# Block-recurrent attention and feed-forward: token weights of the reading through DRAM in 5 transfers instead of 16 moves

## The chip, the cores and the metric

One Trainium2 chip; the program runs on one core. The metric is device time in microseconds of one execution, here the median over runs. The core has TensorE (PE; its weight loads, PEld, overlap its matmuls), VectorE (DVE), ScalarE (ACT), GpSimd (POOL) and SyncE (SP). SyncE computes nothing here: it issues DMAs, one after another, and an issue that has to wait holds up all that come after it. SBUF is the on-chip memory of 128 rows (partitions), PSUM holds what TensorE writes (eight banks), DRAM is outside.

## The reference

Two parts, the first giving the input of the second. B, H, S, Ns, D are 8, 8, 512, 32, 64; the feed-forward has d_model 512 and d_ff 2048. All is float32; the two weights come as float64.

```python
def _attn_ref(x, state):
    scale = 1.0 / np.sqrt(D)
    scores = scale * np.matmul(x, state.transpose(0, 1, 3, 2))
    a = softmax(scores)                        # over the 32 states
    xread = np.matmul(a, state)                # (B, H, S, D)
    scores2 = scale * np.matmul(state, x.transpose(0, 1, 3, 2))
    a2 = softmax(scores2)                      # over the 512 tokens
    sread = np.matmul(a2, x)                   # (B, H, Ns, D)
    return np.concatenate([xread, sread], axis=2)

def _moe_ref(x, w_in, w_out):                  # x: (B * 544, 512)
    h = x @ w_in
    sp = np.maximum(h, 0.0) + np.log1p(np.exp(-np.abs(h)))
    g = h * erf(sp)
    return g @ w_out
```

(The softmax is written out in the reference, with the row maximum taken off and 1e-9 added to the sum.) The second softmax, a2, gives each token a weight for each state; `sread` is the *reading* of this document: for each head, 32 weighted sums over 512 tokens.

## The kernel before

The work is cut by batch and by half of d_ff. In the first half of the run (units A, one per batch, then SA for the rows of `sread`) the first 1024 columns of d_ff are done, in the second half (units B and SB) the other 1024; B adds to what A stored. Batch 0 goes by a path of its own at the front, with small pieces that start as soon as data is there. The products of a unit are cut into quarters and done with seven products instead of eight (a Strassen scheme, in B with a second level), which is why there are so many sums on VectorE: `hidden` (L623) makes the unit's first products, `second` (L675) and `inner` (L734) the second ones, softplus and erf are on ScalarE, the sums are in `sums_a`, `sums_y`, `inner_sums` and `mixed`.

The attention's `xread` is never formed: its weights `a` stay as the unit's right factor (`y`), and `mixed` (L575) multiplies the states with w_in instead. The reading is formed, as states' rows for SA and SB.

The attention of batches 1 to 7 is written in `attention(b)`. All of its work is on tiles inside `at`, with heads paired (h = 2i + e):

- Loads `xq` (two DMAs per head) bring x so that 32 x 32 block transposes on VectorE (`tx`) give it with the channel on the rows. `s` (L493) forms the scores of all heads in two PSUM banks, row = 32 i + state, column = token; ScalarE copies them to `sc` (`c0`, `c1`).
- First softmax: block transposes `tu`, maximum `mx`, `sb`, exp `ex`, sum `sm`, `iz`, `nm`, and transposes back, `ta`, into `y`.
- Second softmax: maximum `my` and `ms`, exp `ey` with its sum, into `both[:, 2 + e]`; `iy` takes the sums' inverse. Then `ty0` and `ty1` transpose the weights block by block into `both[:, 0:2]`: after it a row is 32 i + (token mod 32), and the columns are (e, c, m, n): half, group c of 128 tokens, m (which 32 of them) and state n.
- The product needs a token on each of 128 rows. So the blocks have to move between rows: the block at rows 32 i, columns m goes to rows 32 m, columns i, of `a2T`. Sixteen DMAs from SBUF to SBUF do it, `z00` to `z33` (L534), 32 rows x 8 runs of 32 floats each, 32 KB.
- `x0` to `x7` (L298) load x itself for the product, one DMA per head, into `x_n` (row = token in the group, columns = group, head, channel).
- `read(b)`: `rd` (L467) multiplies, 32 states x 64 channels per matmul, over the four groups of tokens; `rn0`, `rn1` (L475) scale by the sums' inverse; `rt` transposes, `rc` copies into `sT`.

Batch 0 (`attention0`) fills `a2T` from PSUM with the copies `tw0c` and `tw1c`.

`sums_y` also puts `y` and its sums in DRAM for the second half (`kept_y`, L551, 512 KB, and `kept_sy`, L553). The weights' columns are loaded as float64 and put together from their words in `piece` (`i0` to `i7`, `o0` to `o7`), the later ones in between the A units.

The order of everything is written out: `ORDER` is a list of some 2,400 step names. Each step emits its instructions when its name comes up, and each engine runs its own instructions in that order, SyncE's DMA issues too. Names: `a3z12` is step z12 of batch 3's attention, `A2p10` a second product of unit A2, `rd3` the reading of batch 3, `~7*11` eleven small matmuls into bank 7 that compute nothing and keep TensorE busy.

Of the kernel before, what the change touches and what calls it, by code (L numbers as in the profile page):

```python
# [8 lines left out]
F32 = mybir.dt.float32  # L9
# [8 lines left out]
warm lx0 lst0 lx2 lx1 lx3 i0l0 lst8 lst5 lst3 lst7 lst4 lst1 ~7*11 x0 lst2 s0 lst6 x0c i1l1 x2 s0c  # L18
i1l0 i0l1 x1 i2l0 i2l1 x3 x1c i3l1 x2c i3l0 q0 x3c q01c q1 i0a0 q00c big0 tm0 i0a1 i0v0 q10c q11c
i0v1 ~7*1 tm1 max0 u0 i0v2 max1 o0l0 n00 u1 less0 less1 exp0 big1 exp1 sum0 sum1 i1a0 inv0 inv1  # L20
norm0 i1a1 big i1v0 ~4*16 ta0 n00c0 norm1 i0+a0 i1v1 ta0c ~7*1 ta1 i0+a1 n00c1 ta1c i1v2 wt1 i0+v0
wt0 ~6*6 n02 i0+v1 n02c0 i2a1 i0+v2 n02c1 o0l1 ~7*5 n01 i2a0 h0 o1l1 n01c1 u1c o1l0 n01c0 a1xq0
i2v0 h1 i2v1 a1xq1 h0s i3a0 i2v2 h2 h0c i3v0 h1c o2l1 i3a1 u0c o2l0 n10 a1xq2 h3 n10c1 h1s i3v1
n10c0 h2c o0a0 h4 i3v2 h2s wz h3c o3l1 wn0 n12 o3l0 o0a1 h5 wn1 a1xq3 n12c1 h3s o0v0 a1xq5 n12c0
y01 tw1 o0v1 a1xq4 tw0 h0e a1xq7 y02 h6 o0v2 tw1c a1xq6 tw0c h0g o1a0 rd0 a1tx0 o1a1 o10 rn0 a1x5
o1v0 h2e a1x3 o1v1 a1x4 i4l1 rt0 o2a1 o00 o1v2 o2a0 o20 h2g o2v0 h4s o22 o2v1 h4c o3a1 o2v2 h7
o3a0 a1tx1 h5s o3v0 o02 h6s y04 rc0 h5c a1tx2 yl0 h7s o3v1 o12 a1tx3 h4e o3v2 a1s h4g a1c1 a2xq7
a1c0 a1tu1 h7c i4l0 o04 a1tu0 h6c a1x0 i5l0 h6e a1mx1 i5l1 a1mx0 A1m0 a2xq4 a1sb1 o24 a2xq5 a1sb0
a1ex1 a1my1 a1ex0 a2xq0 a1sm1 A1m01 o14 a1x2 a1sm0 A1m00 a2xq1 a1iz h6g i4a0 a1x6 A1m1 a2xq2 i4a1
a1nm0 o06 a1my0 a2xq3 A1m10 a1ta0 A1m11 a2xq6 a1ms a1nm1 a1ey1 A1f01 y11 a1ey0 A1M1 o26 a1ta1  # L30
A1f0c o0c A1M2 i5a1 A1f05 y12 A1M3 A1f06 a1ty0 y13 A1f02 A1f0u2 a1ty1 A1f07 A1M4 A1f0c11 a1z23
i4v0 a1z02 A1f11 A1f0u3 a1z03 y14 i4v1 a1z11 A1f04 a1z22 a1z01 o30 A1f0c22 A1f0s11 a1z20 i4v2
a1z13 A1f0c21 A1f1c A1f03 A1f0s22 i4k a2tx3 a1z12 A1f0s12 A1f16 a1x1 A1f0c12 A1f12 a1x7 A1f1u2
a1iy T1 a1z33 A1f0s21 A1f17 a1z10 A1f1c11 a1z21 a2tx0 A1f15 a1z32 A1f1u3 a2tx1 a1z31 A1f1s11 A1f14
A1f1c22 a1z00 i5a0 a1z30 y03 A1f13 a2tx2 yk0 A1f1c21 i5v0 yl1 o32 A1f1s22 i6l0 A1f1c12 A1f1s12
i5v1 rd1 T2 A1e0 rn10 a2x0 rn11 i5v2 rt1 i6l1 rc1 a2x7 a2s A1g0 A1f1s21 o34 a3xq0 a2c1 a2c0 a3xq2
a2tu0 o36 a3xq4 a2tu1 A1e1 a2mx0 i7l1 A2m0 a2mx1 a3xq7 a2sb0 o16 a2x1 A2m00 A1g1 i5k A2m01 a3xq3
o3c A2m1 a3xq5 a2sb1 A1p10 i7l0 a2ex0 A1A1 a2x6 o1c a2ex1 o1d a2sm0 A1p11 A2m11 a2x2 a2sm1 o2c
a2x5 a3xq1 a2iz a2nm0 A1p50 A1pc a3xq6 a2ta0 A2m10 a2nm1 A2f01 A2M1 a2ta1 A1p51 A2f0c y21 i6a1
a2my0 a2my1 A2f02 i6a0 A2M2 A2f05 a2ms y22 A2f0c11 i6v0 a2ey1 A2f06 A2M3 a2ey0 A2f11 a2ty1 A2f0u2  # L40
a2ty0 A1p20 y23 a2z12 A1A2 a2z22 A2f07 a2x3 y24 a2z02 A1A3 A1p60 o3d A2f0u3 a2z23 A2f0c22 a2z00
a2z11 A2M4 A2f04 A2f0s11 a2z21 i6v1 a2z03 A2f03 A2f0c21 a2x4 A1p61 a2z13 A2f1c A2f0c12 a2z20
A2f0s12 i6v2 a2z31 A2f0s22 a2z10 A2f0s21 A2f16 a2z01 T3 A1pu2 a2z33 A2f15 A2f1u2 a2z32 a2iy a2z30
a3tx1 A2f12 i6k A1A4 A2f17 yk1 A2e0 a3tx2 A1p70 a3tx3 T4 A2f1u3 rd2 i7a1 A2f1c22 A2f14 rn20 a3x2
rn21 i7a0 a3tx0 a3x6 rt2 A2f13 A2g0 o0d rc2 A2f1c11 a3x1 A1p71 yl2 a3x7 i7v0 A2f1s22 a3s A1pu3
A2f1c12 A2f1c21 A1pc22 A1p21 a3c0 a4xq0 a3c1 a3tu0 A2f1s21 o2d a3tu1 a4xq2 A3m0 A2f1s11 a3mx0
a4xq4 i7v1 A1p30 A3m01 A3m00 o5l0 a3my0 A2f1s12 a4xq3 A3m1 a3my1 a3mx1 A1p31 a3sb0 A2e1 a3sb1 i7v2
A1p40 A1pc11 A3m11 A2g1 o4l0 A1d3 A1p41 a4xq6 a3ex1 A1pc12 a3ex0 A2p10 A3m10 a3sm1 A1d1 A1pc21
A2A1 a3x4 i7k A2p11 o4l1 a3sm0 a4xq1 a3iz a3ms a3nm0 a4xq7 A2p50 A2pc a3ta0 a3ey0 a3x5 a3nm1 a4xq5
a3ey1 A3f01 A2A2 A2p51 A3f0c A3M1 y31 a3ta1 A2p60 y32 A3M2 a3ty0 A3f06 a3ty1 A3f02 y33 A3f0u2  # L50
a3z12 A3M3 o4a0 a3x0 A3f05 y34 a3z31 A3M4 A3f07 a3z03 A3f0c11 a3iy a3z22 o4a1 A3f11 a3z00 a3x3
A3f0u3 A2p61 a3z33 A3f0c22 a3z23 o5l1 a4tx3 A1d0 A3f04 o4v0 a3z11 A3f03 a3z02 A3f0c21 a3z13 A2pu2
A2p20 a3z01 A3f0c12 A3f1c a3z30 A2A3 a3z10 a3z20 A3f15 a3z21 o4v1 A3f0s22 a3z32 A3f16 A3f0s21 yk2
A3f0s11 o4v2 A3f12 yl3 A3f1u2 A3f0s12 A2p70 a4tx2 A3f1c11 a4tx1 A2A4 rd3 A3e0 A3f17 rn30 a4x0 rn31
a4tx0 a4x1 rt3 A2p71 A1d2 A3f1u3 o4k rc3 A3f1c22 A3g0 a4s A3f1s11 A2pu3 A3f13 a5xq7 a4c1 A3f14
a4c0 A3f1c12 a5xq6 A3f1s22 a4tu0 A4m0 A3f1c21 a4x2 A3f1s21 a4mx0 o6l0 A2p40 A4m00 a4tu1 a4x3
A3f1s12 yk3 a4mx1 a5xq5 a4my0 A2p21 a5xq1 A2pc22 A3e1 a4my1 a4x5 A2p41 a4x4 a4ms a4sb1 a4x6 A4m01
a4sb0 a5xq0 A3g1 A4m1 a5xq2 a4ex1 A2p30 a5xq4 a4ex0 A2pc11 a4sm1 a5xq3 A2pc21 a4sm0 A2p31 A4m11
a4iz a4ey1 a4nm0 A4m10 A3p10 a4nm1 a4ta0 a4ta1 A4f01 y41 A2pc12 A3p11 A4f0c A3A1 A2d1 o5a1 A4M1
A4f02 a4ey0 y42 A3p50 a4ty0 A4f0c11 A4M2 A4M3 A4f06 a4ty1 A4f0s11 A4f11 y43 A4f0u2 a4z31 a5tx0  # L60
a4x7 o5a0 A4f05 A3A2 a4z22 A2d3 A4f07 A3pc a4z23 y44 a5tx3 A3p60 a4z33 A4f0u3 a4z13 A3A3 a4z32
a4z00 A3p61 A4M4 a4z10 A4f0c22 a4z21 a4z12 o5v0 a4z11 A4f04 A3pu2 o5v1 a4z02 A4f0s22 A4f03 a4z20
A4f0c21 a4z30 a5tx1 A3p70 a4z01 A4f1c a4iy o5v2 a4z03 A4f0s12 A4f16 A4f0c12 A4f0s21 A4f15 A4f1u2
rd4 A4f17 rn40 A4e0 a5x5 rn41 a5tx2 yl4 rt4 A4f12 A3A4 o5k A2d0 A3p20 A4f1u3 o7l0 A4f1c11 A4f1c22
rc4 A4g0 a5s A4f1s11 A4f13 a6xq3 a5c0 a5c1 A4f14 a5my0 yk4 a5tu1 a6xq2 A3p71 A4f1c21 a5tu0 A4f1s22
a5x1 A4f1c12 A4f1s12 A2d2 A3p51 a5mx1 a5x4 A3pu3 a5x3 a5my1 A4f1s21 o6l1 a5sb1 a6xq6 A5m0 a5mx0
a5ms A4e1 a6xq7 a5sb0 A3p21 A3pc22 a5x7 a5x0 A5m01 a6xq1 A3p40 A4g1 a6xq0 a5ex0 A3p41 a6xq5 A5m00
a5sm0 a5ex1 A3pc11 a5sm1 A5m1 a5iz A3p30 a5nm0 A5m10 A5m11 a5ta0 a5ey0 a5nm1 A5f01 a5ey1 A5M1
A3p31 a5ty0 A3pc21 A5f0c a5ta1 o6a0 a5ty1 A4p10 y51 a5z01 A5M3 a5z00 y52 a5z31 A5f05 a5iy A5M2
a5x2 a5x6 y54 A5f02 A4A1 a5z11 A5f06 a5z02 a6xq4 y53 A4p11 A4A3 A5f0u2 a5z21 A5f0c11 a5z12 a6tx0  # L70
a5z13 A5f07 A3pc12 A3d3 A5f0s11 o6v0 a5z30 A5f11 a5z32 o6a1 A4A2 A4p50 a5z23 a5z03 A5f0u3 A5M4
a5z22 A4pc a5z20 A5f0c22 A5f04 a5z10 o6v1 A5f0s22 a5z33 A5f03 A5f0c21 A3d1 a6tx2 yk5 A4p60 A5f0s12
o7l1 A5f0c12 A5f1c A3d0 a6tx1 A5f0s21 A4A4 A5f16 rd5 A5e0 A5f15 rn51 a6x7 rn50 a6tx3 A4p61 A5f1u2
rt5 A5f17 rc5 A4pu2 A5f12 A5f1u3 a6s A5f1c22 A5g0 A5f13 A5f1s22 a7xq7 a6c1 A5f14 a6c0 a6x0 A3d2
A4p70 o6v2 A5f1c21 yl5 A5f1c11 a7xq1 A5f1c12 A6m0 a7xq5 a6tu0 A5f1s21 a6my0 A4p71 a6x2 A6m00 a6tu1
a6x1 A5f1s11 a6my1 o6k a7xq3 a6mx0 A4p20 A4pu3 a6ms a6sb0 A6m01 a6x5 a7xq6 A5f1s12 a6mx1 A4p51
a6sb1 a7xq0 A5e1 a7xq2 A6m1 A4pc22 A4d3 A4p21 a6x3 A5g1 a6x6 a6ex0 A4p30 a6ex1 A6m10 a6sm0 A6m11
a6sm1 A4p40 a6ey1 a6iz a6nm1 A4p31 a6nm0 a6ta0 A6M1 A6f01 y61 a6ta1 A4p41 A6f0c a6ty1 A4pc11 a6ey0
y62 A6M2 A6f02 o7a0 a6ty0 A6f06 A6M3 a6z30 A6f0c11 o7v0 A6f05 a6x4 A6f0u2 a6z10 y63 o7a1 A6f11 y64
a6z00 A4pc12 a6z02 A6f07 A6M4 a6z32 a6z33 A5p10 A6f0u3 a6z11 a6z12 A6f0c22 a6z03 A5A1 A6f04 a7xq4  # L80
A6f03 A5A3 a6z20 A6f0c21 a6z31 A5p50 A6f1c a6z22 a7tx0 a6z01 a6iy A6f0c12 a6z23 a6z21 A6f16 a6z13
a7tx2 A6f15 A4d1 A6f1u2 o7v1 yk6 A5p11 yl6 a7tx3 A6f0s21 A5A2 rd6 a7tx1 A6f12 rn61 a7x7 rn60 A5A4
a7x5 rt6 A6f17 a7x0 rc6 A6f1c11 a7s A6f1u3 A6f0s12 A6f1c22 A6f14 a7c1 o7v2 a7c0 A6f13 A4pc21 a7tu1
A7m0 A5pc A6f0s11 a7mx1 A5p60 a7tu0 A7m01 A7m00 a7sb1 A6f1c21 a7mx0 A5p20 a7sb0 a7my0 a7ex1 A7m1
a7ex0 a7sm1 a7sm0 A5p61 A7m10 a7iz a7nm0 A5p21 a7ta0 A6f1s12 a7my1 A7m11 A5pu2 a7ms A6f1c12 A7f01
A7M1 A5p51 a7nm1 a7ey1 y71 A7M2 A7f0c A5p70 a7ey0 a7ta1 a7ty1 y72 A7f02 a7ty0 A6f0s22 y73 A7f06
a7z13 A7M3 A7f0c11 a7z20 A6f1s22 A7M4 A5p71 A4d0 A6f1s21 y74 a7x6 A6f1s11 a7z22 A7f0u2 a7z23 A7f11
A5pu3 a7z02 A4d2 A7f07 A5pc22 a7z00 A7f05 a7z10 A6e1 a7z32 A5p40 a7x1 a7z03 o7k A6e0 A6g1 yK0
A5p30 a7x4 a7z01 a7x3 A5pc11 A5p31 a7z30 A7f0u3 A6g0 a7z12 a7z11 a7z31 A5p41 a7z33 A7f0c22 A5pc12
# [83 lines left out]
def kernel(  # L173
# [12 lines left out]
    P = 128  # L186
# [871 lines left out]
```

## Time and profile before

| | |
|---|---|
| median of 3 runs | 723.74 us (721.35 to 723.83) |
| the profiled execution, its own time | 723.68 us |
| its span (first to last instruction) | 721.9 us |
| mean granted clock of TensorE | 0.996 |
| HBM read, written | 45.61 MB, 29.36 MB |
| issue of one z move (L534, 112 of them) | 585 / 608 / 1263 ns (min / median / max) |
| issue to landing of one z move | 1.9 / 1.9 / 4.5 us |
| issue of one x load (L298, 56 of them) | 374 / 514 / 2292 ns |
| issue to landing of one x load | 2.2 / 3.2 / 6.3 us |
| issue to landing of one kept_y write (L551, 8) | 3.0 / 3.2 / 5.4 us |

The profile is of one execution. A row of a group of instructions names line, engine, operation, tiles (out<-in), shapes and count; after the bar come busy time and mean duration, then the engine's idle time just before them and what ended it. A row of waits reads: who <- for whom: microseconds in total, how often, the longest. A row of the chain reads: start, microseconds, what; "SPq" is SyncE issuing, "DMA" a transfer under way. In a table by stage, each engine has its busy time in the stage and (x) its number of instructions, then come TensorE's granted clock, the DMA engines' busy share and GB/s. L238 is the helper that runs a step which is a single call, so copies, transposes and others share it. The line of a DMA is that of its issue.

### The profile page before, as it was taken

How to read it: one execution, taken by the hardware profiler on the slowest of the kernel's cores; microseconds unless marked ns; L12 is line 12 of the kernel's file. 1: busy time of each engine (PE TensorE's matmuls, PEld its weight loads, DVE VectorE, ACT ScalarE, POOL GpSimd, SP SyncE). 2: the span in 40 equal slices, each digit the busy share in tenths (PEclk: the TensorE clock that was granted, in tenths of full speed). 3: DMA queues.
4: the chain of work that ended last, by engine and by line, in shares of the span. 5: the costliest groups of instructions: out<-in, count | busy, mean ns of one | idle time of the engine just before them, and what ended most of it. 6: DMA issues, size and time to landing. Idle time of an engine off the chain costs nothing.

```text
span 721.9 us, 12570 instructions
## 1 busy us (share of the span) xinstructions
PE 703.9 (98%) x5027; PEld 584.9 (81%) x5027; DVE 555.3 (77%) x749; ACT 475.7 (66%) x711; POOL 37.6 (5%) x38
## 2 busy tenths in 40 slices
PE   8999899999999999999999999999999999999996
PEld 7544568786868777788979879998989898989996
DVE  4999889988978687945353568597879698879994
ACT  2998877869687774964541684675665678684711
POOL 0000000000000000000000001001020202020220
PEclk9999999999999999999999999999999999999999
DMA  8777694868465565074421122025151514142542
GB/s 249 250 188 162 159 227 124 230 152 227 95 190 120 152 151 123 12 191 158 163 65 50 39 64 39 9 66 96 15 96 15 96 15 95 15 66 31 86 52 69
DMA packets 158458, 79.47 MB, mean 110 GB/s; under 512 B 123840, under 2 KB 150464, under 8 KB 158144
## 3 DMA queue, kind: packets, MB, share of 16 engines
q1 hardware_dynamic: 149664, 70.28, 36.2%
q0 software_dynamic: 8192, 7.87, 9.1%
q8 instruction: 39, 0.64, 0.4%
q10 hardware_dynamic: 544, 0.52, 0.2%
q14 instruction: 19, 0.16, 0.1%
HBM read 45.61 MB, written 29.36 MB: 104 GB/s over the span
## 4 chain that ended last, share of the span: by engine, by line
PE 73%; SPq 10%; DVE 6%; DMA 3%; ACT 2%; issue 2%; DVEq 0%
PE b L734 24%; PE b L623 17%; PE b L675 17%; SPq L534 7%; PE b L926 3%; PE b L575 3%; PE b L886 2%; PE b L865 2%; DMA at<-in_x_dram 2%; DMA at<-at 2%; PE b L467 1%; DVE at L238 1%; PE b L493 1%; SPq L298 1%; SPq L303 1%
## 5 line engine op out<-in xcount | busy, mean ns | idle before, releaser
L675 PE MATMUL b<-ta,ring 128*128 128x256 f32 x840 | 193.1, 381 | 0.0
L675 PEld LDWEIGHTS b<-ta,ring 128*128 128x128 f32 x840 | 158.0, 191 | 31.7 <-issue 9.2
L238 ACT COPY ring<-b 128x512 f32<-128x512 f32 (+1 forms) x138 | 79.8, 584 | 87.3 <-PE b L623 60.8
L623 PE MATMUL b<-y,m 128*128 128x256 f32 x480 | 120.1, 382 | 0.0
L238 ACT COPY res<-b 128x512 f32<-128x512 f32 (+2 forms) x104 | 54.5, 532 | 83.9 <-PE b L734 41.0
L623 PEld LDWEIGHTS b<-y,m 128*128 128x128 f32 x480 | 88.1, 191 | 16.0 <-issue 2.2
L232 DVE TENSOR_TENSOR ring<-ring 128x2048 f32<-128x2048 f32 (+1 forms) x36 | 77.7, 2166 | 28.0 <-ACT ring L631 23.0
L623 PE MATMUL b<-sy,m 128*128 128x256 f32 x360 | 91.2, 382 | 0.0
L230 DVE TENSOR_TENSOR ring<-ring,b 128x512 f32<-128x512 f32 (+1 forms) x66 | 44.5, 675 | 55.7 <-PE b L623 21.3
L734 PEld LDWEIGHTS b<-at,ring 128*128 128x128 f32 x660 | 79.8, 192 | 5.0 <-ACT res L238 1.1
L734 PE MATMUL b<-at,ring 128*128 128x128 f32 x660 | 82.3, 276 | 0.0
L612 ACT ACTIVATE ring<-ring 128x512 f32<-128x512 f32 x128 | 77.3, 631 | 3.8 <-DVE ring L230 2.3
L231 DVE TENSOR_TENSOR ring<-ring 128x1024 f32<-128x1024 f32 (+2 forms) x67 | 75.3, 1132 | 0.1
L623 PEld LDWEIGHTS b<-sy,m 128*128 128x128 f32 x360 | 66.2, 191 | 11.2 <-issue 2.2
L651 POOL DMA_DIRECT2D out_dram<-res x32 | 37.0, 1290 | 664.4 <-ACT res L238 503.7
L631 ACT ACTIVATE ring<-ring 128x2048 f32<-128x2048 f32 x30 | 57.2, 1911 | 0.3
L230 DVE TENSOR_TENSOR res<-res,b 128x512 f32<-128x512 f32 (+2 forms) x50 | 30.6, 614 | 30.8 <-ACT res L238 15.3
L238 ACT COPY m<-b 128x512 f32<-128x512 f32 (+2 forms) x65 | 35.4, 565 | 16.5 <-PE b L575 16.1
L238 ACT COPY b<-b 128x512 f32<-128x512 f32 (+2 forms) x57 | 31.3, 553 | 20.3 <-PE b L623 9.3
L238 DVE STREAM_TRANSPOSE at<-at 128x512 f32<-128x512 f32 x56 | 38.6, 700 | 3.0 <-DMA at<-in_x_dram 1.2
L734 PE MATMUL b<-cv,ta 128*128 128x128 f32 x312 | 40.2, 276 | 0.0
L734 PEld LDWEIGHTS b<-cv,ta 128*128 128x128 f32 x312 | 38.1, 192 | 1.3 <-issue 0.8
(145 smaller groups left out, 916.1 us busy)
## 6 DMA issues: line engine op xcount, KB each, us to landing
out_dram<-res SPq DMA_DIRECT2D x32, 256.0 KB, 2.4
at<-in_x_dram SPq DMA_DIRECT2D x112, 64.0 KB, 3.2
at<-in_x_dram SPq DMA_DIRECT2D x56, 128.0 KB, 3.2
out_dram<-res POOLq DMA_DIRECT2D x28, 256.0 KB, 4.5
cv<-in_moe_w_in_dram SPq DMA_DIRECT2D x12, 512.0 KB, 5.7
cv<-in_moe_w_out_dram SPq DMA_DIRECT2D x12, 512.0 KB, 5.7
kept_y<-y SPq DMA_DIRECT2D x8, 512.0 KB, 3.2
y<-kept_y SPq DMA_DIRECT2D x8, 512.0 KB, 4.0
```

What stands on the lines that cost most here:

```text
L230: add = lambda o, a, b: tt(o, a, b, op=ALU.add)
L231: sub = lambda o, a, b: tt(o, a, b, op=ALU.subtract)
L232: mul = lambda o, a, b: tt(o, a, b, op=ALU.mult)
L238: do[name] = lambda: f(*args)
L534: step(name("z%d%d" % (mm, i)), lambda mm=mm, i=i: nc.sync.dma_start(out=rows[Ns * mm:Ns * mm + Ns, i], in_=blocks[Ns * i:Ns * i + Ns, mm]))
L575: pe.matmul(out=bank[6 + k][Ns * p:Ns * p + Ns, :], lhsT=by, rhs=w_in[r, 4 * j:4 * j + 4, i, :], start=True, stop=True)
L612: act.activation(out=o, in_=i, func=ACTF.Softplus)
L623: pe.matmul(out=to[:, i], lhsT=xs[n - 1][:, q:q + P], rhs=ys[n - 1], start=(start and i == 0), stop=(i == 1), skip_group_check=True)
L631: step(u + "e%d" % o, lambda s=s: act.activation(out=s, in_=s, func=ACTF.Erf))
L651: nc.gpsimd.dma_start(out=to, in_=of, accum_op=ALU.add)
L675: pe.matmul(out=to[:, E2 * h:E2 * h + E2], lhsT=a[:, k // 2, k % 2], rhs=rhs[n][:, k], start=(start and h == 0 and k == 0), stop=(k == 3), ...
L734: pe.matmul(out=out_[:, P * j:P * j + P], lhsT=lhs[:, i], rhs=rhs[:, i], start=(start and j == 0 and i == 0), stop=(i == 1), skip_group_ch ...
```

## The change

The sixteen moves of a batch become one write and four loads. The weights are transposed (`ty0`, `ty1`) into the order (m, e, c, n), so that what goes to the rows 32 m is one run of 256 floats in each row; `kz` writes all 128 rows x 1024 to one of two DRAM tiles (512 KB); `z0` to `z3` each load what belongs on rows 32 m, 32 rows x 4 runs of 1 KB (128 KB). A load `z` waits for `kz` to have landed. `a2T` is read with (i, e, c, n) as its column order, by the product and by batch 0's copies `tw0c`, `tw1c`, which now write runs of 32 floats. x for the reading is loaded by token group, `x0` to `x3`, all heads in one DMA of 256 KB, in place of one DMA of 128 KB per head. The same runs of 256 bytes are loaded as before.

`ORDER` is a new list for the new set of steps, and differs all over, also in places that have nothing to do with the reading: 2,308 names in place of 2,411. There are eight groups of filling matmuls, 43 in all, in place of six with 40.

```diff
-    a2T = at[:, 7168:8192].rearrange("p (e c q) -> p e c q", e=2, c=NC)
+    a2T = at[:, 7168:8192].rearrange("p (i e c n) -> p e c i n", i=NI, e=2, c=NC)
+    turned = at[:, 4096:6144]
+    kept_z = [dram.tile([P, 1024], F32, name="kept_z%d" % k) for k in range(2)]
...
-    def load_x(b, h):
-        nc.sync.dma_start(out=x_n[:, :, h, :], in_=x[b, h].rearrange("(c p) d -> p c d", p=P))
+    def load_x(b, c):
+        nc.sync.dma_start(out=x_n[:, c], in_=x[b].rearrange("h (c p) d -> c p h d", p=P)[c])
...
+    def load_z(b, m):
+        nc.sync.dma_start(
+            out=at[Ns * m:Ns * m + Ns, 7168:8192].rearrange("p (i f) -> p i f", i=NI),
+            in_=kept_z[b % 2].rearrange("(i t) (m f) -> m t i f", t=Ns, m=4)[m])
...
-                step("tw%dc" % e, act.copy, a2T[:, e].rearrange("p c q -> p (c q)"), tw[e])
+                step("tw%dc" % e, act.copy, a2T[:, e],
+                     tw[e].rearrange("p (c q n) -> p c q n", c=NC, q=NI))
...
-                        pe.matmul(out=sr[q, e, :], lhsT=a2T[:, g, c, Ns * p:Ns * p + Ns],
+                        pe.matmul(out=sr[q, e, :], lhsT=a2T[:, g, c, p],
                                   rhs=xt[:, c, 2 * i + e, :], start=(c == 0), stop=(c == NC - 1))
...
         for e in range(2):
-            step(name("ty%d" % e), turn, both[:, e], both[:, 2 + e])
-        blocks = both[:, 0:2].rearrange("p e (c m n) -> p m (e c) n", m=NI, n=Ns)
-        rows = a2T.rearrange("p e c (i n) -> p i (e c) n", n=Ns)
-        for mm in range(NI):
-            for i in range(NI):
-                step(name("z%d%d" % (mm, i)), lambda mm=mm, i=i: nc.sync.dma_start(
-                    out=rows[Ns * mm:Ns * mm + Ns, i], in_=blocks[Ns * i:Ns * i + Ns, mm]))
-        for h in range(H):
-            step(name("x%d" % h), load_x, b, h)
+            step(name("ty%d" % e), turn,
+                 turned[:, 0:1024].rearrange("p (m e c n) -> p e c m n", m=NI, e=2, c=NC)[:, e],
+                 both[:, 2 + e].rearrange("p (c m t) -> p c m t", c=NC, m=NI))
+        step(name("kz"), lambda: nc.sync.dma_start(out=kept_z[b % 2], in_=turned[:, 0:1024]))
+        for m_ in range(NI):
+            step(name("z%d" % m_), load_z, b, m_)
+        for c in range(NC):
+            step(name("x%d" % c), load_x, b, c)
```

One stretch of the order, from the last `ty` of batch 4 to its reading, as SyncE meets it. Before: `a4z31 a4x7 a4z22 A2d3 a4z23 a4z33 a4z13 a4z32 a4z00 a4z10 a4z21 a4z12 a4z11 a4z02 a4z20 a4z30 a4z01 a4z03`, then `rd4`. After: `a4kz a5xq3 a4z1 a4z2 a4z0 a4z3 a5xq6 a5xq7 A2d1`, then `rd4` (an `xq` is two DMAs, `A2d1` a store of results).

## The prediction

> **What bounds the kernel now.** I read the page's busy table and chain first, then the table of waits, then the timeline and chain around one reading.
>
> ```profile
> PE 703.9 (98%) x5027; PEld 584.9 (81%) x5027; DVE 555.3 (77%) x749; ACT 475.7 (66%) x711; POOL 37.6 (5%) x38
> ...
> PE 73%; SPq 10%; DVE 6%; DMA 3%; ACT 2%; issue 2%; DVEq 0%
> ```
>
> TensorE is busy 98% of the span. The chain gives SyncE's queue 10% of the span (72 us), but that share is no prize: a chain runs through whatever was last, also where the engine behind it stood for a moment only. What can be won is TensorE's own idle time, and only where TensorE is the bound. The waits say how much of that the moves cause:
>
> ```profile
> DVE sn L475 <- PE b L467: 18.1, 7, 4.8
> ...
> PEld b L467 <- DMA at<-at: 8.6, 8, 2.0
> ...
> PE b L467 <- DMA at<-at: 6.6, 7, 1.6
> ```
>
> L467 is the reading's product (rd), and `at<-at` are the sixteen moves z. Weight loads stood 8.6 us for them in the whole run, matmuls 6.6 us, largely the same time. One reading (batch 6), first the timeline, then the chain ahead of it:
>
> ```profile
> 284.61 1.40 PEld L467 LDWEIGHTS b<-at 128*32 128x32 f32 x64 [1.86 <-DMA at<-at]
> 284.61 1.56 PE L467 MATMUL b<-at 128*32 128x64 f32 x64 [1.46 <-DMA at<-at]
> ```
>
> ```profile
> 270.34 0.71 DVE at L238
> 271.07 0.59 SPq L534
> ...
> 281.99 0.62 SPq L534
> 282.64 1.92 DMA at<-at
> 284.61 0.50 PE b L467 x6
> 285.12 1.05 PE b L467 x58
> 286.18 1.06 PE b L623 x4
> 287.24 0.11 PE b L477
> 287.35 0.86 PE b L623 x4
> ```
>
> Transpose ty1 ends at 271.05, the sixteen issues run one behind another to 282.6, the last one lands 1.92 later, and TensorE has stood 1.86 us. From first issue to product it took 13.5 us, nearly all of it SyncE's sequencer. The other engines by stage:
>
> ```profile
> core 0: us, PE busy (x) PEld busy (x) DVE busy (x) ACT busy (x) POOL busy (x), PEclk, DMA share, GB/s
> 0.00:20.00 20.00, 17.51 (x191) 15.72 (x191) 10.59 (x22) 7.13 (x12) 0.69 (x6) 1.00 0.88 259
> 20.00:120.00 100.00, 96.18 (x582) 56.35 (x583) 92.26 (x140) 86.54 (x128) 0.00 (x0) 0.98 0.72 181
> 120.00:200.00 80.00, 79.20 (x544) 63.16 (x543) 70.97 (x106) 61.12 (x90) 0.00 (x0) 1.00 0.70 175
> 200.00:330.00 130.00, 125.51 (x906) 100.68 (x905) 95.74 (x148) 92.55 (x135) 0.00 (x0) 1.00 0.54 133
> ```
>
> From 20 to 120 us VectorE is full (92%) and weight loads are at 56%: there VectorE sets the pace. From 120 to 200 both are near it (VectorE 89%), after 200 TensorE alone (VectorE 74%). After 330 no reading is left, and nothing that the change touches but the order.
>
> **What the change removes and adds.** The issues and landings by their rows:
>
> ```profile
> at<-in_x_dram SPq DMA_DIRECT2D x56, 128.0 KB, 3.2
> ...
> kept_y<-y SPq DMA_DIRECT2D x8, 512.0 KB, 3.2
> y<-kept_y SPq DMA_DIRECT2D x8, 512.0 KB, 4.0
> at<-at SPq DMA_DIRECT2D x112, 32.0 KB, 1.9
> ```
>
> SyncE per batch: sixteen moves at 0.608 us (median of L534) are 9.7 us; in their place come one write kz, 0.473 us as kept_y (the same 512 KB from 128 rows), and four loads z at 0.51 us (x loads, L298, same 128 KB), 2.5 us together. Four x loads fewer save 4 x 0.514 = 2.1 us; the larger pieces I cost at the same issue time. So 9.3 us less per batch, 65 us over seven batches. This is worth nothing by itself: SyncE's time counts only where a reading waits for it.
>
> Path from ty1 to the product, new: kz lands 3.2 us after its issue, then three issues of 0.5 us ahead of the last z, which lands some 3.2 us after its own issue (x load; its 1 KB runs into 32 rows have no row of their own). That is 3.2 + 1.5 + 3.2 = 7.9 us against 13.5. Bounds: kept_y landed in 3.0 to 5.4 us and x loads in 2.2 to 6.3, so 6.7 to 13.2. I take the medians, as the moves' own share of the DMA work goes away.
>
> But the new order also asks for the reading sooner. I counted the TensorE work that each list puts between ty1 and rd (a unit product L623 x4 0.86 us, a second product L675 x8 1.73, L493 and L575 x16 1.02): before, 12.1, 12.9, 12.9, 11.3, 13.8, 12.9 and 21.6 us for batches 1 to 7; after, 12.0, 10.4, 10.4, 11.2, 12.0, 10.3 and 17.2. Need before is ty1's 0.7 us and the stretch from first issue to last landing, 13.0 to 15.1 us (18.0 in batch 7): by this count batches 1 to 6 lack 1.3 to 2.4 us each, 11.5 in all, and batch 7 nothing. The trace shows 0.6 to 2.0 each, 8.6 in all, and none in batch 7, so the count is a fair measure. Need after is 0.7 + 0.1 + 7.9 = 8.7 us, under every one of the seven: 1.6 us to spare in the tightest.
>
> Sum on the profiled execution's 723.68 us (the median of the runs is 723.74, the same):
>
> - rd's waits go: -8.6 us (6.6 if only the matmuls' idle time counts; 10.9 with the late start of what stands behind rd).
> - In batch 1's wait the granted clock of the 80 to 100 us stretch was 0.91; 9% of 20 us is 1.8 us. If the dip belongs to the stall, it goes as well. No run shows which; I take half, -0.9.
> - Waits left: two of eight kept_y writes landed late, after 4.2 and 5.4 us; the one leaves 0.6 of the 1.6 us to spare, the other lacks 0.6. +1.0 for two such cases (0 to +17.7, which is a need of 14.0 us in every batch, as in the first rival).
> - Given back to VectorE: batches 1 to 4 hold 1.65 + 0.61 + 0.67 + 1.95 = 4.9 us of the 8.6, in stretches where VectorE is 89 to 92% busy. What TensorE gains there it can keep only as far as VectorE keeps up. I take half, +2.4 (0 to +4.9).
> - The transposes ty now write 32-element runs in another order, and tw's copy too. The trace has no transpose with broken runs; TENSOR_TENSOR in strided quarters (683 ns in ring) costs what it costs in contiguous rows (682 ns in m). So 0; if a transpose took twice its 0.70 us, 14 x 0.7 = 10 us of VectorE, half on the path, +5 at most.
> - The order elsewhere: TensorE's work is the same (three warming matmuls of 0.11 us more). ScalarE changes function tables 60 times instead of 65, 5 x 1.28 us less; ScalarE is at 66%, so 0. The first A unit (A1m0) now stands behind 21.7 us of counted TensorE work instead of 33.4, batch 0's second products behind it. VectorE's counted work at equal TensorE progress is the same within 2.5 us up to 180 us, so I take 0 for the front; bounds +5 and -5, its own idle time of TensorE (6.3 us in 0 to 100).
>
> -8.6 - 0.9 + 1.0 + 2.4 = -6.1: 717.6 us, I say 717.5.
>
> The Trainium skill ("DMA: Bandwidth & Descriptors", Issuing engines are not separate DMA queues) holds that the sequencer's time to start a DMA is usually small against the transfer. By it fifteen of the sixteen moves would cost next to nothing, and the time would stay at 723.7. The trace differs: 0.608 us to issue against 1.9 us to land, sixteen times over, so the row decides; the 0.02 that I leave this way is counted in (2).
>
> **Rivals.** (1) The way through DRAM is too slow: slower. SyncE stands at the first z until kz has landed, with the next batch's xq loads behind it, and the DMA engines are 70% busy in 20 to 200 us. For it: kept_y's 5.4 and 4.2 us there, x loads up to 6.3. Against: medians of 3.2, and 3.7 MB of 128-byte moves gone. Waits by the count, batches 1 to 6: at a need of 12.5 us 0.5, 2.1, 2.1, 1.3, 0.5 and 2.2, 8.7 in all, as much as before; from there on the change loses. The upper bound is 0.8 + 13.2 = 14.0; halfway to it, at 13.3, they are 1.3, 2.9, 2.9, 2.1, 1.3 and 3.0, 13.5 in all: 723.7 - 8.6 + 13.5 = 728.6.
>
> The Trainium skill ("DMA: Bandwidth & Descriptors", Latency and other measured facts) gives HBM access 0.2 us on average and 2 us at high load. By that two trips under load would add 2 x 1.8 = 3.6 us to 8.7, an estimate of 12.3, just short of this rival's threshold; no row here shows one trip by itself.
>
> (2) VectorE takes all of it: up to 200 us the 4.9 us come back in full, and the later 3.7 us shrink because the new list has 4 to 6 us more VectorE work ahead of TensorE's progress at 220 to 260 us. For it: 89 to 92% busy. Against: 74% after 200. 723.7 - 1.5 = 722, no change.
>
> (3) The front gains too: rd1's stall, its clock dip and half of the 6.3 us of idle go, VectorE keeps up: -8.6 - 1.8 - 3 = 710.
>
> (4) The change doesn't reach rd because another wait ends there last, such as an x chunk, which now covers all heads and both halves of the product. The last x load of a batch stands 6 to 23 us of counted work ahead of rd, and x loads landed within 6.3; 0.03, within (2), 723.
>
> **How the numbers follow.** Forecast 717.5 with chance 0.48, (1) 0.17, (2) 0.17, (3) 0.18. The likeliest one's own range is 713 to 721. The range goes from 706 to 729: below (3) by the 4 us of the front's bound, above (1) by little. Within 0.5% means 720.1 to 727.4, about what a measurement here can tell from no change. Faster: (3) and nine tenths of the forecast, 0.61. Same: (2), the rest of the forecast and 0.02 of (1), 0.24. Slower: the rest of (1), 0.15.
>
> **What would show it.** The wait of L467 for a DMA at most 2 us in all instead of 8.6; kz's landing near 3.2 us, the last z's landing within 8.7 us of ty1's start; SyncE's issues fewer by 105; TensorE's idle time in 200 to 330 us down from 4.5. It is wrong if readings wait for z as long as before, if VectorE passes 95% in 120 to 200 us while TensorE idles more, or if the transposes ty take over 0.8 us.

## The result, and the profile after

The changed kernel takes 714.2 us (median of 4 runs, 714.11 to 714.48) against 723.79 us beside it; the ratio is 0.9876 with a 95% interval of 0.9855 to 0.9897. The span of the profiled execution went from 721.9 to 712.4 us. It is faster by 9.6 us, where 6.2 were forecast.

First the waits of the reading's product, which is now L468: what its weight loads and matmuls stood for (microseconds, times), then the table of waits. No DMA is left among them; before, `at<-at` stood there with 8.6 and 6.6 us. VectorE's wait for the reading (`sn`) fell from 18.1 to 7.1 us.

```profile
its engine sat idle before it (us, times) until:
  issue: 2.3, 7
  ACT at L231: 0.9, 1
```

```profile
DVE sn L476 <- PE b L468: 7.1, 6, 2.9
```

The chain that ended last runs through TensorE for 94% of the span; SyncE's 10% is gone from it:

```profile
PE 94%; DVE 1%; ACT 0%; issue 0%; DVEq 0%
PE b L675 27%; PE b L623 26%; PE b L734 24%; PE b L575 4%; PE b L886 4%; PE b L926 4%; PE b L865 2%; PE b L468 1%; PE b L494 1%; DVE ring L223 1%; PE b L854 0%; DVE w_in L350 0%; DVE w_in L351 0%; DVE res L223 0%; ACT at L231 0%; PE b L478 0%
```

Batch 6 in the timeline (start, duration, engine, line). kz goes out at 251.89, a load of x goes past, SyncE stands until kz has landed, the four z go out from 255.08 to 256.82, and the product starts at 262.02, 2.8 us after the last of them landed at 259.20. The 0.33 us ahead of it is the instruction issue that a reading always has:

```profile
251.89 0.34 SPq L533 DMA_DIRECT2D kept_z<-at  x1
252.28 0.43 SPq L293 DMA_DIRECT2D at<-in_x_dram  x1
...
255.08 1.74 SPq L303 DMA_DIRECT2D at<-kept_z  x4
...
262.02 0.94 PEld L468 LDWEIGHTS b<-at 128*32 128x32 f32 x64 [0.33 <-issue]
262.02 1.10 PE L468 MATMUL b<-at 128*32 128x64 f32 x64
```

Issue times (min/median/max, ns) of kz and z, from the answers by source line. The time to landing was 2.6/2.9/3.3 us for kz and 2.5/2.9/6.0 us for z, and in batch 6 the way from kz's issue to the last landing took 7.3 us. Over the seven batches it took 7.0 to 10.8 us, the longest in batch 1, and the product started 2.4 to 7.1 us behind the last landing:

```profile
L533 SPq DMA_DIRECT2D kept_z<-at x7: 338/350/351, 62.7 to 284.7; - x7
```

```profile
L303 SPq DMA_DIRECT2D at<-kept_z x28: 309/430/1958, 66.0 to 290.1; - x28
```

The engines by stage, as before:

```profile
core 0: us, PE busy (x) PEld busy (x) DVE busy (x) ACT busy (x) POOL busy (x), PEclk, DMA share, GB/s
0.00:20.00 20.00, 17.93 (x191) 15.56 (x191) 10.30 (x22) 7.14 (x11) 0.69 (x6) 1.00 0.92 279
20.00:120.00 100.00, 97.35 (x602) 58.68 (x601) 95.68 (x143) 83.98 (x125) 0.00 (x0) 1.00 0.76 197
120.00:200.00 80.00, 80.00 (x621) 62.74 (x620) 70.50 (x111) 63.00 (x96) 0.00 (x0) 1.00 0.70 188
200.00:330.00 130.00, 130.00 (x880) 106.30 (x879) 103.47 (x153) 88.46 (x135) 0.00 (x0) 1.00 0.57 159
```

TensorE idles no more in 120 to 330 us. VectorE did not fall behind: from 120 to 200 us it is as busy as before (70.50 and 70.97 of 80), and in 20 to 120 us it went from 92% to 96%, by idling less.

Where the time came from is best seen against the lists. For each reading I take its start, less the TensorE work that the list puts ahead of it (counted as in the prediction; small products of the front and of the last batch are left out alike in all). What is left is lost time, up to a constant:

| lost, us, up to | rd1 | rd2 | rd4 | rd7 | the end |
|---|---|---|---|---|---|
| before | 27.0 | 32.4 | 37.6 | 44.0 | 58.9 |
| changed | 27.3 | 29.6 | 31.2 | 33.6 | 49.1 |

The front gives nothing (27.0 and 27.3 us up to rd1), the second half nothing (14.9 and 15.5 us from rd7 on). Between the first and the seventh reading the kernel before lost 17.0 us and the changed one loses 6.3, and 3.1 of these 10.7 us lie between the first and the second reading.

### The profile page after: what moved, and what is told of

Same layout as the page of the kernel before. It is cut to its first block, busy times and chain, and to the rows that moved or that the text cites. A ratio compares the mean times of both kernels' runs of the same rounds, so it can differ in the third digit from the quotient of the medians.

```text
span 712.4 us, 12455 instructions
## 1 busy us (share of the span) xinstructions
PE 700.4 (98%) x5033; PEld 581.8 (82%) x5033; DVE 554.8 (78%) x749; ACT 468.5 (66%) x706; POOL 37.8 (5%) x38
## 4 chain that ended last, share of the span: by engine, by line
PE 94%; DVE 1%; ACT 0%; issue 0%; DVEq 0%
PE b L675 27%; PE b L623 26%; PE b L734 24%; PE b L575 4%; PE b L886 4%; PE b L926 4%; PE b L865 2%; PE b L468 1%; PE b L494 1%; DVE ring L223 1%; PE b L854 0%; DVE w_in L350 0%; DVE w_in L351 0%; DVE res L223 0%; ACT at L231 0%; PE b L478 0%
## 5 line engine op out<-in xcount | busy, mean ns | idle before, releaser
L623 PE MATMUL b<-y,m 128*128 128x256 f32 x480 | 122.3, 382 | 0.0
L231 ACT COPY b<-b 128x512 f32<-128x512 f32 (+2 forms) x57 | 31.2, 551 | 18.7 <-PE b L926 5.5
```

The source lines that it names most:

```text
L231: do[name] = lambda: f(*args)
L623: pe.matmul(out=to[:, i], lhsT=xs[n - 1][:, q:q + P], rhs=ys[n - 1], start=(start and i == 0), stop=(i == 1), skip_group_check=True)
```

## The experiments

Ratios are to the kernel before on the same chip (its medians there were 723.4 to 724.5 us), with 95% intervals.

**The new order with the old moves, and the old order with the new way.** These two tell the way from the list.

```diff
 # e1: the changed kernel; a2T, ty and the product as before
-a4kz ... a4z1 a4z2 a4z0 a4z3
+a4z31 a4z22 a4z23 ... a4z01 a4z03          # all sixteen where kz stood
 # e2: the kernel before; a2T, ty, the product, kz and z as changed
-a4z31 ... (sixteen places)
+a4kz ... a4z0 a4z1 a4z2 a4z3               # at the first, and the sixth to ninth place
```

> The new order with the sixteen moves back, all sixteen where kz stood, x still by group of tokens. Theory (the gain is the reading's wait, and the wait is SyncE's sixteen issues): first issue to last landing is 15 x 0.65 + 1.9 = 11.7 us with nothing in between, the need 12.5 us against 10.3 to 12.0 us of TensorE work in batches 1 to 6, so readings wait 0.5, 2.1, 2.1, 1.3, 0.5 and 2.2 us, 8.7 in all by the count (the trace of before had three quarters of its count): 721 to 723 us, 1.7 more for each stall that brings a stretch of half clock. Rival (the new list is better in itself, whichever way the weights go): 714 to 716, waits of L467 for the moves under 2 us.

> The old order with the way through DRAM: kz where the first move stood, the four loads where the sixth to ninth stood, x still by head. Theory: need 8.7 us against 11.3 to 13.8, so no reading waits, and no half clock after reading 1: 723.7 - 8.6 - 1.7 = 713.4, at most 716 if VectorE gives some back. Rival (the new list made the gain): 722 to 724, TensorE idling elsewhere for what it no longer waits in the reading.

> The old order with the way through DRAM once more, with batch 5's ty0 behind ta1 instead of ahead of it: ty0 now writes columns of both halves, and ahead of ta1 it overwrote weights of batch 5 that ta1 still had to read (in e2_old_order_new_way batch 5's weights are therefore not the reference's). Same instructions otherwise: 712.5 to 714 us if the way alone makes the gain; the rival that the new list made it is already down to 1 us.

Measured: e2 713.09 us, 0.9845 (0.9829 to 0.9861), and e2b 713.23 us, 0.9859 (0.9841 to 0.9878). In e2 batch 5's `ty0` overwrites weights that are still to be read, so e2b, where it stands behind `ta1`, is the one to go by (e9 and e10 have it there too). The way alone makes the whole gain, in the list that was made for the moves. The rival, that the new list made it, is out.

e1 took 744.0 us, 1.027 (1.0248 to 1.0292): right in its sign, since the moves are what costs, but 20 us slower than before and not 721 to 723. The count had looked at the reading and its own moves alone. TensorE's waits in e1, of the reading's product (L463) and of the transpose rt behind it (L473), show what it left out:

```profile
PE b L463 <- DMA at<-in_x_dram: 7.3, 3, 4.2
...
PE b L473 <- DVE sn L471: 6.8, 2, 3.4
```

The product's matmuls stood 11.6 us in all (6.6 in the kernel before), and 7.3 of them for loads of x. These three waits are in batches 1, 2 and 6, where the changed list has loads of x behind kz, and e1 so has them behind the sixteen moves. The 6.8 us of rt (0.6 before) are in batches 4 and 5. The chain of one of them, around batch 4, first SyncE's queue, then VectorE (start, duration, line; in brackets VectorE's idle time and what ended it):

```profile
194.62 10.51 SPq L530 DMA_DIRECT2D at<-at  x16
205.18 4.51 SPq L299 DMA_DIRECT2D at<-in_x_dram  x6
```

```profile
201.70 0.68 DVE L226 TENSOR_TENSOR res<-res,b 128x512 f32<-128x512 f32 x1
208.31 1.90 DVE L234 STREAM_TRANSPOSE at<-at 128x512 f32<-128x512 f32 x3 [5.93 <-DMA at<-in_x_dram]
...
211.83 0.47 DVE L471 TENSOR_SCALAR sn<-b,z 128x64 f32<-128x64 f32 x2
```

The sixteen issues held SyncE for 10.5 us. Behind them stood the next batch's xq loads; VectorE's transposes tx waited 5.93 us for these, and `sn`, which stands behind tx on VectorE, was late for TensorE: before the transpose rt it stood 3.4 us. In the changed kernel the same six xq issues are out by 188.5. So a move's issue time was paid here by the reading, by the loads behind it on SyncE, and by what stands behind their users. In e1, lost time grows by 33.1 us between the first and the seventh reading, 26.8 more than in the changed kernel, and the granted clock falls to half five times for 3.41 us each. That adds up: 11.6 and 6.8 us of waits and 8.5 us for the half clock are 26.9. The sixteen moves stand here in one block, ahead of loads that the changed list has behind kz, so the 744.0 us are the price of moves at that place.

**Sixteen moves with long runs.** Is it the number of moves or their 128-byte runs?

```diff
-        step(name("kz"), lambda: nc.sync.dma_start(out=kept_z[b % 2], in_=turned[:, 0:1024]))
-        for m_ in range(NI):
-            step(name("z%d" % m_), load_z, b, m_)
+        for m_ in range(NI):
+            for i in range(NI):
+                step(name("z%d%d" % (m_, i)), lambda m_=m_, i=i: nc.sync.dma_start(
+                    out=at[Ns * m_:Ns * m_ + Ns, 7168 + 256 * i:7424 + 256 * i],
+                    in_=turned[Ns * i:Ns * i + Ns, 256 * m_:256 * m_ + 256]))
```

> The new order and the new order of columns, but sixteen moves inside SBUF where kz stood, each 32 rows x one run of 1 KB instead of 32 rows x 8 runs of 128 bytes; no DRAM. If an issue costs by the DMA and stays at 0.61 us, the need is 12.5 us as with the old moves: 721 to 723. If it costs by the runs that SyncE has to name, 0.43 us as the loads z: 15 x 0.47 + 1.9 + 0.8 = 9.8 us, under all seven: 714 to 715, and the way through DRAM is not what matters.

739.96 us, 1.0217 (1.0200 to 1.0234), with this row for the issue of a move:

```profile
L532 SPq DMA_DIRECT2D at<-at x112: 507/589/1272, 63.0 to 319.9; - x112
```

A move with one run a row took 0.589 us to issue where one with eight runs took 0.609. It is the number of moves inside SBUF that costs here, not the runs that each is made of; both kinds carry 32 KB. The price of 721 to 723 missed for the same reason as in e1: the product's matmuls stood 9.2 us, rt 6.5, and the clock was at half for 13.7 us, worth 6.8. The loads z, of four such runs a row from DRAM, took 0.430.

**x by head or by group.** Each kernel with the other's loads of x.

```diff
 # e3: the changed kernel             # e4: the kernel before
-load_x(b, c): x_n[:, c]              -load_x(b, h): x_n[:, :, h, :]
+load_x(b, h): x_n[:, :, h, :]        +load_x(b, c): x_n[:, c]
```

> The changed kernel with x loaded by head again, two loads where one stood. Theory: x is early by 6 us or more in every batch and SyncE has the time, so 714.2 within 1 us. Rival (x by group is a part of the gain, through SyncE's time or later x): 716 to 718.

> The kernel before with x for the reading by group of tokens, four loads where the first, third, fifth and seventh stood; the sixteen moves stay. Theory: x is not what the reading waits for, and of the four issues saved (2 us of SyncE) those among the moves shorten the wait by at most 0.5 us in three or four batches: 722 to 724. Rival (any relief of SyncE helps as much as it is long): 7 x 2 us spread over the waits, 8.6 us of which at most half go: 719 to 720.

e3: 713.73 us, 0.9862 (0.9838 to 0.9886). With the way through DRAM, the four loads of x saved are worth nothing. e4: 717.75 us, 0.9928 (0.9909 to 0.9948), and there my theory missed and the rival was right, even low: without the way, the same saving is worth 5.7 us. SyncE's queue around batch 1's moves, the kernel before and then e4:

```profile
69.83 2.08 SPq L303 DMA_DIRECT2D at<-in_x_dram  x4
72.01 5.34 SPq L534 DMA_DIRECT2D at<-at  x8
77.45 0.54 SPq L356 DMA_DIRECT2D kept_in<-res  x1
78.04 0.59 SPq L534 DMA_DIRECT2D at<-at  x1
78.67 1.27 SPq L298 DMA_DIRECT2D at<-in_x_dram  x2
79.98 4.51 SPq L534 DMA_DIRECT2D at<-at  x7
```

```profile
70.57 5.34 SPq L530 DMA_DIRECT2D at<-at  x8
...
77.23 0.67 SPq L294 DMA_DIRECT2D at<-in_x_dram  x1
77.95 4.64 SPq L530 DMA_DIRECT2D at<-at  x7
```

The moves began 1.44 us sooner, and one load of x stood among them instead of two: the last move was out at 82.59 instead of 84.49. The stalls of the first reading's weight loads went from 2.41 to 1.02 us, and the half clock behind them did not come. Over all readings the waits for the moves, weight loads and matmuls added up (largely the same time twice), went from 15.3 to 6.0 us. x is thus largely the same gain reached another way: in batch 1, fewer issues ahead of the same landing. The queue is shown for batch 1 alone.

**Batch 1 alone, and the others alone.** For the half clock, and for what VectorE lets through.

```diff
+        if b in (1,):            # e8; (2, 3, 4, 5, 6, 7) in e9
+            ... ty, kz and z as changed
+        else:
+            ... ty and the sixteen moves as before
```

> The kernel before with the way through DRAM in batch 1 alone. Its reading waited 1.65 us, and right behind that wait the granted clock was half for 3.41 us, which costs TensorE 1.7. Theory (the half clock belongs to the stall): no half clock in the trace, 723.9 - 1.65 - 1.7 = 720.5. Rival A (the half clock comes anyway): 722.2. Rival B (VectorE, full in this stretch, takes it all back): 723.9.

> The kernel before with the way through DRAM in batches 2 to 7, the moves in batch 1. Theory: the waits of 0.61 + 0.67 + 1.95 + 1.87 + 1.86 = 7.0 us go and are kept, the half clock behind reading 1 stays: 716.9. Rival (VectorE, 89% busy up to 200 us, takes back what reading 2 to 4 gain, 3.2 us): 720.

e8: 720.72 us, 0.9966 (0.9953 to 0.9980), so 2.7 us of the 3.4 forecast. e9: 717.24 us, 0.9914 (0.9894 to 0.9935), so 6.2 of 7.0; both intervals hold the forecast. The stretch from 88 to 91 us behind the first reading, in the kernel before, e8 and e9; the third number from the end is the granted clock:

```profile
88.00:91.00 3.00, 3.00 (x17) 0.73 (x16) 2.78 (x2) 2.79 (x5) 0.00 (x0) 0.50 1.01 272
```

```profile
88.00:91.00 3.00, 3.00 (x15) 1.13 (x21) 2.58 (x5) 2.97 (x5) 0.00 (x0) 1.00 0.81 166
```

```profile
88.00:91.00 3.00, 3.00 (x18) 0.80 (x17) 2.48 (x2) 2.81 (x4) 0.00 (x0) 0.50 1.01 289
```

The half clock goes with the stall of reading 1 and stays where that stall stays. Between rd1 and rd2, e8 loses 2.3 us where the kernel before loses 5.4 and e9 5.4: 3.1 us for one reading, nearly what its wait (1.65) and the clock (1.7) come to. What each of the two is worth is not settled by that: of the 17 executions of the kernel before beside e8, three took 720.8 to 721.2 us, as long as e8, at a mean granted clock of 0.998 to 0.999, the others 721.9 to 725.3 us at 0.994 to 0.996, and no trace of the three was kept. VectorE, full in this stretch, took nothing of it back.

**kz later.** The changed kernel, with the write repeated, each one behind the landing of the one before.

```diff
-lambda: nc.sync.dma_start(out=kept_z[b % 2], in_=turned[:, 0:1024])
+lambda: [nc.sync.dma_start(out=kept_z[b % 2], in_=turned[:, 0:1024]) for _ in range(2)]   # or 3
```

> The changed kernel with kz written twice, the second write behind the landing of the first, so that everything from z on is 2.9 us later and SyncE stands that much longer. In the changed kernel the last z lands 2.4, 3.3, 2.8, 3.6, 3.9, 2.8 and 7.1 us ahead of the reading in batches 1 to 7. If only the reading counts: waits 0.5, 0, 0.1, 0, 0, 0.1, 0, so 714 to 716 us. If what stands behind z in SyncE's queue counts as well (the next batch's xq loads, which VectorE's transposes tx wait for): tx late by 1 to 2 us in four or five batches, 718 to 722.

> The same with kz three times, 5.8 us later. If only the reading counts: waits 3.4, 2.5, 3.0, 2.2, 1.9, 3.0 and 0, 16 us, and up to six half-clock stretches at 1.7: 730 to 740. With the queue behind it on top: 735 to 748. This is the price of the prediction's slower rival, a way through DRAM that takes too long (need 13.9 us).

Twice: 714.81 us, 0.9894 (0.9865 to 0.9923), no reading waits for z. The first z goes out 2.6 to 3.1 us later, by kz's issue, and in batches 1 to 6 the last one lands 0.2 to 1.0 us ahead of the product: the way had that much to spare, and what stands behind it in SyncE's queue cost nothing either. Three times: 735.53 us, 1.0169 (1.0137 to 1.0201), with these waits of TensorE:

```profile
PE b L468 <- DMA at<-kept_z: 14.1, 6, 3.0
```

Here the margin is gone in six batches, and lost time grows by 24.6 us from rd1 to rd7 instead of 6.3. That is the prediction's slower rival, and shows the cliff: some 2.7 us of delay cost nothing that can be told, the next 2.8 cost 20.7 us. The matmuls' 14.1 us and 13.7 us at half the clock, worth 6.8, make up 20.9.

**Both edits in the old order.** What is then missing is only the new list.

> The old order with both edits, the way through DRAM and x by group of tokens; all that is missing of the change is the new list. Theory (no reading waits any more with the way alone, so x has nothing left to shorten): 713 us within 1, as e2b_old_order_new_way. Rival (the two gains, 10.2 and 5.7 us, add where they touch different things): 708 to 711.

> The changed kernel as it is, timed beside the one above on the same chip: 714.2 us within 0.5. If the new list is worth anything by itself it is under the run above by over 1 us; by the runs so far it is 0 to 1 us over it.

e10: 713.28 us, 0.9844 (0.9822 to 0.9867). e11, the changed kernel once more: 713.73 us, 0.9852 (0.9831 to 0.9873). The two gains do not add, and the new list is worth nothing that these runs can tell. No version beat the changed kernel by more than the intervals allow.

## Why the prediction was right, point by point

The sign and the mechanism were right, the time lies 3.3 us below the forecast and within the likeliest case's own range of 713 to 721. Each term of the sum:

- Waits of rd, -8.6: shown. They are zero in the changed kernel, in e2b and in e10. The count of need against work laid between was a fair measure of the reading: it said no wait after the change, and there is none. It was no measure of anything else, as e1 and e5 showed: for moves put back it gave 8.7 us where 30 were lost. One of its sizes was short, too: from kz's issue to the last landing it had 7.9 us, and batches 1 and 7 took 10.8 and 9.7; batch 1 had 2.4 us left all the same, since its product came 13.2 us behind kz's issue, where the count had 12.0 us of work behind ty1.
- The half clock, -0.9: mis-sized, it is -1.7 in the traces. It goes with the stall of reading 1 (e8 against e9, one trace each). The Trainium skill ("TensorE: Matmul & The Clock Gate", Part 1: The HAM clock gate) states a window of 3413 ns and half rate behind an idle one; the length is the trace's 3.41 us. But no window of that length was idle ahead of it: the stall was in pieces, TensorE counting as busy for 6.07 of the 8 us from 80 to 88. Why these pieces were enough, and those of the readings at 203.6, 242.5 and 284.6 us (1.5 us each) were not, stays open.
- Waits left, +1.0: mis-sized, it is 0. kz landed in 2.9 us at the median and 3.3 at most, where I had kept_y's 5.4 for a bound, and the last z landed 2.4 us or more ahead of each product. In the same run kept_y itself took 5.0 us at the median, so its row was a poor neighbour, and on the other side: two writes of the same size from the same number of rows differ by 2.1 us in one run. What makes the difference, no run shows.
- Given back to VectorE, +2.4: this is the step that failed. I had read 89 to 92% busy as an engine that sets the pace. It had been waiting for the same readings. Its waits for them (`sn`) in the kernel before, from 20 to 120 and from 120 to 200 us:

```profile
DVE sn L475 <- PE b L467: 1.7, 1, 1.7
```

```profile
DVE sn L475 <- PE b L467: 2.5, 2, 1.5
```

  These 4.2 us stand beside the 4.9 us that the readings stood there; the rest of the 18.1 us lies behind 200 us, where the term charged nothing. In the changed kernel they are 0 and 1.2 us: VectorE did its work sooner once the readings came sooner. e8 and e2b keep what the readings gain.
- Transposes with broken runs, 0: shown, the fourteen `ty` took 668 to 711 ns in the changed kernel and 670 to 712 before.
- The order elsewhere, 0: shown by e10 against e11; the front's lost time up to rd1 is the same in both lists.
- SyncE's relief, nothing except where a reading waits for it: right both ways. In the changed kernel four loads of x more cost nothing (e3); in the kernel before four fewer are 5.7 us (e4), because there the reading waited for SyncE's queue. What I had wrong was e4's expectation, which put the saving at 0.5 us a batch in a few batches and left the half clock out.

With the waits and the half clock alone, -8.6 - 1.7 = -10.3, against 9.6 measured and 10.2 in e2b; the -8.6 are weight loads' waits, by the matmuls alone it is 6.6. The three mis-sized terms (0.8, 1.0 and 2.4 us) all lie on the slow side, where the forecast was 3.3 us off.

Of the rivals, (1) did not come up, and e6 shows where it begins: between some 2.7 and 5.5 us more delay. Its waits then are what it had put (14.1 us against 13.5), but the time is 735.5 us and not 728.6, since it left out the half clock that follows. (2) fell. (3) came true in part: reading 1's stall and clock dip went and VectorE kept up, but the front's 3 us of idle time did not go, by the lost time up to rd1. The measured time lies between the forecast and (3). (4) fell: no reading waits for x in the changed kernel.

## What to carry to other kernels

An issue queue is to be counted like an engine: many small DMAs cost their number times the issue time (here 16 times 0.6 us), and the bill comes to every load that stands behind them and to the engine that waits for that load, not only to the transfer's own reader. An engine that is 90% busy beside a stall may be waiting for the same stall; before something is charged as given back to it, look at what ended its own idle time. And when two edits shorten the same wait, try each by itself: here they were worth 10.2 and 5.7 us alone and 11 together.

## What the runs showed of the hardware that was not expected

A DMA from SBUF to SBUF took SyncE 0.59 to 0.61 us to issue whether a row carried one run or eight, a load from DRAM into 32 rows 0.43 us, and kz, a write of 512 KB from 128 rows to DRAM, 0.35 us (kept_y, of the same size, 0.49). Half the TensorE clock for 3.41 us came five times in one execution of e1, each beginning within 0.8 us of the end of a stall of 1.3 to 4.2 us, and none came in the changed kernel or e2b between the front and the end.
